# A grouped-query decode attention plus token mixer: ring of load buffers at multiples of 512 bytes, one output-weight load no longer split, values loaded right behind the next keys, the last two heads' output weights loaded last

## The chip, the cores and the metric

The kernel runs on one NeuronCore of a Trainium2 chip. The metric is the device time of one execution in microseconds (us). Several executions are timed; the median of three executions of the kernel before is 1326.07 us (1325.22 to 1327.07). One further execution is recorded by the hardware profiler. Engines are named as the profile names them: PE is the matrix engine (PEld its weight loads), DVE the vector engine, ACT the scalar engine, POOL the general engine, and SP the engine whose queue issues nearly all DMA transfers. All data is float32.

## The reference, cut to what matters

```python
B, Sq, D = 8, 1, 512
Hq, Hkv, Sk, Dh = 32, 8, 8192, 128          # k_cache, v_cache: (B, Hkv, Sk, Dh)
x = A_x
xn = _layernorm(x)
q = (xn @ wq).reshape(B, 1, 32, 128).transpose(0, 2, 1, 3)
k = jnp.repeat(k_cache, 4, axis=1)
v = jnp.repeat(v_cache, 4, axis=1)
p = softmax(einsum("bhqd,bhkd->bhqk", q, k) * 128 ** -0.5)
a = einsum("bhqk,bhkd->bhqd", p, v).transpose(0, 2, 1, 3).reshape(B, 1, 4096) @ wo
h = _layernorm(xn)                            # mixer: tokens axis has length 1
u = gelu(einsum("bsd,sf->bdf", h, w1) + b1)   # F = 1792
y = einsum("bdf,fs->bds", u, w2) + b2
return x + a + y.transpose(0, 2, 1)
```

Each of the 64 pairs of a key/value head h (8) and a batch b (8) has 4 MiB of keys and 4 MiB of values, and four query rows. The caches alone are 537 MB (512 MiB), wq and wo are 8 MiB each.

## The kernel before

The 64 pairs are numbered i = 8h + b, and one pass of `slot(i)` (line 361) works on one pair. A pair's keys, and likewise its values, are one tile `raw` of 128 partitions x 64 rows x 128 numbers (32 KiB in each partition, 4 MiB in all). These tiles live in the pool `ring`, which has five buffers that are used in turn: the sixth tile takes the first buffer, and its load can be issued only when the last reader of the old tile is done. In the text K62 means the keys of pair 62, V62 its values.

**What sets the order of the loads.** Lines 51 to 57 sort a list `order`: keys of pair i at 2i, values at 2i + 1, but for the last two pairs at 2i + 2.5. So the loads stand as K0, V0, K1, V1, ... V61, K62, K63, V62, V63. `load_next` (line 67) takes the next entry and issues it on SP's queue. It is called when a pair's keys have been used (end of `qk`, line 224) and when its values have been used (end of `pv`, line 271). SP works in order: an issue that waits for a buffer holds back those behind it. K0 and K63 are loaded in four pieces, V63 in four pieces of falling size, everything else in one.

**The output weights.** `wo` for head h (1 MiB, `load_wo`, line 83) is a tile of its own of 8 KiB per partition, loaded in the slot with b = 2 of head h. Head 6 is loaded in two transfers, partitions 0 to 7 and partitions 8 to 127 (line 87). Head 7 is loaded behind everything else, in four transfers (lines 79 and 91).

**A slot.** `qk(i)` is 16 matrix products (32 PE rows in the profile, since one float32 product runs as two) of the transposed keys with the placed queries W. DVE transposes the next pair's keys in four quarters, `turn(i + 1, ...)` (line 209), with the softmax of pair i between them: `sm_max` (DVE), `sm_bias` (PE and DVE), `sm_exp` (ACT), `sm_place` (PE, then DVE writes PT). PE does `pv(i - 1)` right behind `qk(i)`, then `o_pick` (three DVE operations that keep the right quarter and add it up) and `o_place` (PE, into the PSUM tile MH of the head). At b = 0 the previous head's result is scaled (`o_sums`, `o_scale`) and multiplied with wo (`o_project`, line 303). The mixer runs beside it on ACT and POOL (`mx_step`), and `mx_end` brings its sum in through PE.

**The end.** Slots 0 to 62 run in the loop; pair 63 is written out by hand from line 399: qk, softmax, pv(62), its pick and place, `o_sums`, pv(63), pick and place, scale, `o_project(7)`, and the store of `yacc`.

**Where the ring lies.** The pool `const` lies in front of the ring in each partition. In the built program the ring's first buffer begins at byte 36,736, which is 128 bytes past a multiple of 256 and 384 past a multiple of 512; the others follow at steps of 32,768.

## Time and profile before

| What | Before |
|---|---|
| Time, median of 3 | 1326.07 us |
| Time of the profiled execution | 1324.89 us |
| Its span (first to last instruction) | 1323.1 us |
| Busy: PE, DVE, ACT, POOL | 790.6, 806.1, 289.0, 230.9 us |
| Loaded by SP's queue (q1) | 553.67 MB in 24,331 packets |
| Mean granted clock of PE | 0.76 |

The span is 1.8 us shorter than the time of the same execution. Four views are used: the page with its 40 slices of 33.08 us each and its groups, the windows (busy time and DMA rate in chosen stretches), the chain of waits, and the timeline of the end. A row of the timeline gives start, duration, engine, source line, operation, output and inputs, how many instructions were merged, and in brackets the idle time in front and what ended it. In a row of the chain stand start, duration and what ran or was waited for. In the windows' rows stand the window, its length, the busy time and count of each engine, the granted clock, the mean busy share of the 16 DMA engines, and GB/s.

### The profile page before, as it was taken

Reading aid. Unit: us, or ns where it says so; the run is one execution under the profiler, and the core shown is the slowest. Engines: PE = TensorE matmul, PEld = TensorE weight load, DVE = VectorE, ACT = ScalarE, POOL = GpSimd, SP = SyncE. Lnnn points to the kernel's source line nnn. Section 1 sums busy time; section 2 is a strip of 40 time slices with the busy share of each in tenths; the row PEclk is TensorE's granted clock in tenths of the full one; section 3 lists DMA queues with packets and bytes.
Section 4 is the critical chain, followed back from the end, with each engine's and each line's share of the span. In section 5 each row is a group of like instructions: output and inputs, shape, how many; then the busy total and the mean of one; then the engine's idle time right before and its main releaser. Section 6 shows DMA issues by size and latency. Waiting matters only on the chain.

```text
span 1323.1 us, 12383 instructions
## 1 busy us (share of the span) xinstructions
PE 790.6 (60%) x5172; PEld 260.9 (20%) x5172; DVE 806.1 (61%) x835; ACT 289.0 (22%) x364; POOL 230.9 (17%) x244
## 2 busy tenths in 40 slices
PE   3366456655577466655467556576466663657566
PEld 2111112111121111211112111121112111122112
DVE  2655765746755666755755756655766736666563
ACT  0023212213212212213212213023221312213220
POOL 1022120212112121112112122022120221203310
PEclk9687786887777787787776776777776886767879
DMA  9999999999999999999999999999999999999993
GB/s 397 437 432 427 429 427 434 432 427 429 432 430 430 427 432 431 431 424 432 432 431 427 429 430 427 434 422 429 432 429 428 433 342 429 435 430 420 432 423 126
DMA packets 24530, 554.50 MB, mean 419 GB/s; under 512 B 2547, under 2 KB 2579, under 8 KB 6939
## 3 DMA queue, kind: packets, MB, share of 16 engines
q1 hardware_dynamic: 24331, 553.67, 98.2%
q8 instruction: 41, 0.67, 0.2%
q14 instruction: 14, 0.11, 0.0%
q0 software_dynamic: 128, 0.02, 0.0%
q10 hardware_dynamic: 16, 0.02, 0.0%
HBM read 553.69 MB, written 0.02 MB: 418 GB/s over the span
## 4 chain that ended last, share of the span: by engine, by line
DMA 53%; PE 22%; DVE 16%; issue 4%; ACT 4%; SPq 0%; ACTq 0%; DVEq 0%
DMA raw<-in_A_k_cache_dram 53%; DVE raw L212 13%; PE s L222 13%; PE misc L253 5%; ACT L246 2%; DVE mr L232 2%; ACT t2k L246 1%; PE misc L317 1%; PE misc L307 1%; PE misc L295 1%; PE o L266 1%; DVE t2k L277 1%; DVE sq L240 0%; PE mh L288 0%; DVE ob L280 0%
## 5 line engine op out<-in xcount | busy, mean ns | idle before, releaser
L212 DVE STREAM_TRANSPOSE raw<-raw 128x2048 f32<-128x2048 f32 x256 | 582.1, 2294 | 380.1 <-DMA raw<-in_A_k_cache_dram 380.1
L222 PE MATMUL s<-raw,w 128*32 128x512 f32 x2048 | 322.2, 785 | 17.0 <-issue 11.8
L328 POOL TENSOR_SCALAR g<-g,w2t 128x512 f32<-128x512 f32 x112 | 77.6, 693 | 921.8 <-ACT g L327 921.8
L266 PE MATMUL o<-raw,pt 128*32 128x512 f32 x2048 | 231.0, 592 | 0.0
L288 PE MATMUL mh<-sel,ob 128*128 128x4 f32 x128 | 35.6, 349 | 322.1 <-DVE ob L281 322.1
L246 ACT ACT_TABLE_LOAD x55 | 70.6, 1283 | 611.6 <-DVE nb L240 611.4
L329 POOL TENSOR_TENSOR macc<-macc,g 128x512 f32<-128x512 f32 x112 | 144.3, 1288 | 9.4
L253 PE MATMUL misc<-t2k,perm 128*128 128x512 f32 x128 | 125.4, 1080 | 15.6 <-ACT t2k L246 15.6
L222 PEld LDWEIGHTS s<-raw,w 128*32 128x32 f32 x2048 | 76.8, 143 | 275.5 <-issue 262.8
L237 PE MATMUL misc<-ident,mr 128*128 128x128 f32 x128 | 33.2, 343 | 146.1 <-DVE mr L232 146.1
L327 ACT ACTIVATE g<-hb,b1t,w1t 128x512 f32<-128x512 f32 x112 | 91.1, 813 | 128.7 <-POOL macc L329 128.0
L288 PEld LDWEIGHTS mh<-sel,ob 128*128 128x128 f32 x128 | 30.0, 291 | 336.6 <-DVE ob L281 336.6
L266 PEld LDWEIGHTS o<-raw,pt 128*32 128x32 f32 x2048 | 62.2, 110 | 157.8 <-issue 157.8
L246 ACT ACTIVATE t2k<-s,nb 128x512 f32<-128x512 f32 x64 | 44.0, 687 | 201.5 <-DVE nb L240 200.9
L255 DVE STREAM_TRANSPOSE pt<-misc 128x512 f32<-128x512 f32 x64 | 45.6, 712 | 39.7 <-PE misc L253 39.6
L327 ACT ACT_TABLE_LOAD x54 | 69.3, 1283 | 1.4
L237 PEld LDWEIGHTS misc<-ident,mr 128*128 128x128 f32 x128 | 20.2, 198 | 203.5 <-DVE mr L232 196.8
L232 DVE TENSOR_REDUCE mr<-s 128x1 f32<-128x512 f32 x64 | 42.0, 657 | 13.4 <-PE s L222 13.4
L277 DVE TENSOR_TENSOR t2k<-o,dm 128x512 f32<-128x512 f32 x64 | 43.9, 685 | 6.3 <-PE o L266 6.3
L205 DVE COPY w<-qt 32x128 f32<-32x128 f32 x64 | 37.1, 617 | 0.7
L253 PEld LDWEIGHTS misc<-t2k,perm 128*128 128x128 f32 x128 | 30.8, 299 | 20.0 <-ACT t2k L246 20.0
L280 DVE TENSOR_TENSOR ob<-t2k 128x256 f32<-128x256 f32 x64 | 27.2, 425 | 2.2
(67 smaller groups left out, 197.5 us busy)
## 6 DMA issues: line engine op xcount, KB each, us to landing
raw<-in_A_v_cache_dram SPq DMA_DIRECT2D x63, 4096.0 KB, 28.9
raw<-in_A_k_cache_dram SPq DMA_DIRECT2D x62, 4096.0 KB, 22.6
raw<-in_A_wq_dram SPq DMA_DIRECT2D x2, 4096.0 KB, 17.1
raw<-in_A_k_cache_dram SPq DMA_DIRECT2D x8, 1024.0 KB, 24.3
wo<-in_A_wo_dram SPq DMA_DIRECT2D x6, 1024.0 KB, 29.9
raw<-in_A_v_cache_dram SPq DMA_DIRECT2D x1, 2048.0 KB
raw<-in_A_v_cache_dram SPq DMA_DIRECT2D x1, 1024.0 KB, 25.8
raw<-in_A_v_cache_dram SPq DMA_DIRECT2D x2, 512.0 KB, 26.8
```

Source lines behind the costliest of these rows:

```text
L212: nc.vector.transpose(t, t)
L222: nc.tensor.matmul(S[i][g * Q:(g + 1) * Q, :], W[h % 2][:, b, j, :], kt[:, g, :, j * Q:(j + 1) * Q], start=(j == 0), stop=(j == NB - 1))
L232: nc.vector.tensor_reduce(mr, S[i], AX.X, ALU.max)
L237: nc.tensor.matmul(m[:, :P], st[i].to_broadcast([P, P]), ident, start=True, stop=True)
L246: nc.scalar.activation(p, S.pop(i), AF.Exp, bias=st[i], scale=SCALE, accum_out=LR[h % 2][:, b:b + 1])
L253: nc.tensor.matmul(m, perm, st.pop(i), start=True, stop=True)
L266: nc.tensor.matmul(O[i][c * Q:(c + 1) * Q, :], PT[i][:, u * Q:(u + 1) * Q], VR[i][:, u * NG:(u + 1) * NG, :].rearrange("p t d -> p (t d)") ...
L277: nc.vector.tensor_tensor(om.rearrange("p (g d) -> p g d", g=NG), O.pop(i).rearrange("p (g d) -> p g d", g=NG), dm.unsqueeze(2).to_broadca ...
L288: nc.tensor.matmul(MH[h][:, b * REP:(b + 1) * REP], OB.pop(i)[:, :DH], sel, start=True, stop=True)
L327: nc.scalar.activation(g, hb, AF.Gelu_apprx_tanh, bias=b1t[:, j:j + 1], scale=w1t[:, j:j + 1])
L328: nc.gpsimd.tensor_scalar(g, g, w2t[:, j:j + 1], 1.0, op0=ALU.mult, op1=ALU.mult)
L329: nc.gpsimd.tensor_add(acc, acc, g)
```

## The change

The load order becomes K0, K1, V0, K2, V1, ... with every pair's values behind the next pair's keys; near the end it is V60, K62, K63, V61, V62, V63. K63 is no longer cut in four. The output weights of heads 6 and 7 are no longer loaded into the `wo` tile: behind V63 they go into one ring buffer, in eight transfers of 256 KiB, and `o_project(6)` leaves slot 56 and is joined to `o_project(7)` at the end. The split load of head 6 goes with that. Pair 62 leaves the loop: the end is written out by hand for pairs 62 and 63, with pv(61), pv(62) and pv(63) behind qk(63). The last pair's pick and place become `o_last`: half of O copied by DVE and half by ACT, then four products with `selg`, a new constant that holds the pick and the place together. `mx_end` of the last head moves from slot 62 to slot 61. Two constants come in front of the ring, `selg` (64 bytes per partition) and `pad` (64 bytes, set to zero and read by nothing), so that the ring begins at byte 36,864 = 72 x 512.

```diff
--- before.py
+++ after.py
@@ -27,6 +27,7 @@
 SCALE = DH ** -0.5
 N_IT = B * HKV
 RING = 5
+PAD = 16
 
 
 @with_exitstack
@@ -51,8 +52,8 @@
     KR, VR = {}, {}
     order = []
     for i in range(N_IT):
-        order.append((2 * i, kc, KR, i))
-        order.append((2 * i + (1 if i < N_IT - 2 else 2.5), vc, VR, i))
+        order.append((2 * min(i, N_IT - 1.9), kc, KR, i))
+        order.append((2 * i + 2.5, vc, VR, i))
     order.sort(key=lambda o: o[0])
     order.reverse()
     WQ = []
@@ -71,24 +72,24 @@
             t = ring.tile([P, NT, DH], F32, name="raw")
             rows = src[b, h].rearrange("(p t) d -> p t d", p=P)
             at = 0
-            for n in (NT // 4,) * 4 if to is KR and i in (0, N_IT - 1) else (NT // 2, NT // 4, NT // 8, NT // 8) if not order else (NT,):
+            for n in (NT // 4,) * 4 if to is KR and i == 0 else (NT // 2, NT // 4, NT // 8, NT // 8) if not order else (NT,):
                 nc.sync.dma_start(t[:, at:at + n, :], rows[:, at:at + n, :])
                 at += n
             to[i] = t
-            if not order:
-                load_wo(HKV - 1)
+        elif HKV - 1 not in wos:
+            t = ring.tile([P, NT, DH], F32, name="raw")
+            t = t.rearrange("p (h r c) d -> p h r (c d)", h=4, r=REP)
+            for h in (HKV - 2, HKV - 1):
+                rows = wo[h * REP * DH:(h + 1) * REP * DH, :].rearrange("(r p) n -> p r n", p=P)
+                wos[h] = t[:, h % 2]
+                for r in range(REP):
+                    nc.sync.dma_start(wos[h][:, r, :], rows[:, r, :])
 
     wos = {}
 
     def load_wo(h):
         t = one.tile([P, REP, D], F32, name="wo")
-        rows = wo[h * REP * DH:(h + 1) * REP * DH, :].rearrange("(r p) n -> p r n", p=P)
-        if h < HKV - 1:
-            for p in (slice(0, 8), slice(8, P)) if h == HKV - 2 else (slice(0, P),):
-                nc.sync.dma_start(t[p], rows[p])
-        else:
-            for r in range(REP):
-                nc.sync.dma_start(t[:, r, :], rows[:, r, :])
+        nc.sync.dma_start(t, wo[h * REP * DH:(h + 1) * REP * DH, :].rearrange("(r p) n -> p r n", p=P))
         wos[h] = t
 
     load_wq()
@@ -126,6 +127,8 @@
                           ident.rearrange("p (g i x) -> p i g x", i=NB, g=NG))
     dm = const.tile([P, NG], F32, name="dm")
     nc.vector.tensor_reduce(dm, ident.rearrange("p (c g x) -> p g c x", c=NB, g=NG), AX.XY, ALU.add)
+    selg = const.tile([P, NG, REP], F32, name="selg")
+    nc.vector.tensor_tensor(selg, sel.unsqueeze(1).to_broadcast([P, NG, REP]), dm.unsqueeze(2).to_broadcast([P, NG, REP]), ALU.mult)
     rj = const.tile([P, NB, NB, Q], F32, name="rj")
     nc.vector.tensor_copy(rj, ident.rearrange("p (j d) -> p j d", j=NB).unsqueeze(2).to_broadcast([P, NB, NB, Q]))
     epst = const.tile([B, 1], F32, name="epst")
@@ -146,6 +149,9 @@
         nc.vector.memset(t, 0.0)
         OTS.append(t)
         LR.append(const.tile([P, B], F32, name=f"lr{k}"))
+
+    pad = const.tile([P, PAD], F32, name="pad")
+    nc.vector.memset(pad, 0.0)
 
 
 
@@ -287,6 +293,16 @@
             MH[h] = ps_h.tile([P, 512], F32, name="mh")
         nc.tensor.matmul(MH[h][:, b * REP:(b + 1) * REP], OB.pop(i)[:, :DH], sel, start=True, stop=True)
 
+    def o_last(i):
+        om = t2k.tile([P, 512], F32, name="t2k")
+        o = O.pop(i)
+        nc.vector.tensor_copy(om[:, :256], o[:, :256])
+        nc.scalar.copy(om[:, 256:], o[:, 256:])
+        b = i % B
+        for g in range(NG):
+            nc.tensor.matmul(MH[i // B][:, b * REP:(b + 1) * REP], om[:, g * DH:(g + 1) * DH], selg[:, g, :],
+                             start=(g == 0), stop=(g == NG - 1))
+
     RD = {}
 
     def o_sums(h):
@@ -300,12 +316,15 @@
         nc.vector.tensor_tensor(OTS[h % 2].rearrange("p r (b s) -> p r b s", s=BS)[:, :, :, 0],
                                 MH.pop(h)[:, :REP * B].rearrange("p (b r) -> p r b", r=REP), RD.pop(h), ALU.mult)
 
-    def o_project(h):
-        m = misc()
-        for r in range(REP):
-            for j in range(NB):
-                nc.tensor.matmul(m[j * Q:(j + 1) * Q, :D // NB], OTS[h % 2][:, r, :], wos[h][:, r, quarter[j]],
-                                 start=(r == 0), stop=(r == REP - 1))
+    def o_project(*hs):
+        m = misc()
+        n = 0
+        for h in hs:
+            for r in range(REP):
+                n += 1
+                for j in range(NB):
+                    nc.tensor.matmul(m[j * Q:(j + 1) * Q, :D // NB], OTS[h % 2][:, r, :], wos[h][:, r, quarter[j]],
+                                     start=(n == 1), stop=(n == REP * len(hs)))
         nc.vector.tensor_add(yacc, m[:, :D // NB], yacc)
 
 
@@ -380,26 +399,39 @@
             if h:
                 o_sums(h - 1)
                 o_scale(h - 1)
-                o_project(h - 1)
+                if h + 1 < HKV:
+                    o_project(h - 1)
         k = 2 if h + 1 < HKV else 3
         for j in range(k * b, min(k * b + k, NF)):
             mx_step(h, j)
-        if b == 2 and h + 1 < HKV:
+        if b == 2 and h + 2 < HKV:
             load_wo(h)
         if 3 <= b < 3 + NB and h + 1 < HKV:
             q_place(h + 1, b - 3)
-        if b == (B - 1 if h + 1 < HKV else B - 2):
+        if b == (B - 1 if h + 1 < HKV else B - 3):
             mx_end(h)
 
     for a in range(4):
         turn(0, a * quart)
-    for i in range(LAST):
+    for i in range(LAST - 1):
         slot(i)
     h = HKV - 1
+    qk(LAST - 1)
+    turn(LAST, 0)
+    sm_max(LAST - 1)
+    turn(LAST, quart)
+    sm_bias(LAST - 1)
+    sm_exp(LAST - 1)
+    turn(LAST, 2 * quart)
+    sm_place(LAST - 1)
+    turn(LAST, 3 * quart)
     qk(LAST)
     sm_max(LAST)
     sm_bias(LAST)
     sm_exp(LAST)
+    pv(LAST - 2)
+    o_pick(LAST - 2)
+    o_place(LAST - 2)
     sm_place(LAST)
     pv(LAST - 1)
     o_pick(LAST - 1)
@@ -407,10 +439,9 @@
     o_sums(h)
     for u0, u1 in ((0, 8), (8, 12), (12, 14), (14, 16)):
         pv(LAST, u0, u1)
-    o_pick(LAST)
-    o_place(LAST)
+    o_last(LAST)
     o_scale(h)
-    o_project(h)
+    o_project(h - 1, h)
     nc.sync.dma_start(out.rearrange("b s (j n) -> j (b s) n", j=NB), yacc[::BS, :])
 
 
```

The first place is SP's queue at the start of the program; `raw` is a buffer of the ring, with the tile's number. Before:

```order
L64 DMA raw_86<-in_A_wq_dram 128x8192
L75 DMA raw_96<-in_A_k_cache_dram 128x2048 x4
L75 DMA raw_101<-in_A_v_cache_dram 128x8192
L75 DMA raw_103<-in_A_k_cache_dram 128x8192
L75 DMA raw_349<-in_A_v_cache_dram 128x8192
L75 DMA raw_351<-in_A_k_cache_dram 128x8192
```

And of the change:

```order
L65 DMA raw_86<-in_A_wq_dram 128x8192
L76 DMA raw_96<-in_A_k_cache_dram 128x2048 x4
L76 DMA raw_101<-in_A_k_cache_dram 128x8192
L76 DMA raw_103<-in_A_v_cache_dram 128x8192
L76 DMA raw_353<-in_A_k_cache_dram 128x8192
L76 DMA raw_355<-in_A_v_cache_dram 128x8192
```

K1 now stands ahead of V0, and so on to the end of the list. With five buffers, K of pair i + 2 used to take the buffer of V of pair i - 1, and now V of pair i + 1 takes that of K of pair i.

The second place is the end of SP's queue, from the keys of pair 61 on. Before:

```order
L75 DMA raw_4735<-in_A_k_cache_dram 128x8192
L75 DMA raw_4758<-in_A_v_cache_dram 128x8192
L75 DMA raw_4808<-in_A_k_cache_dram 128x8192
L75 DMA raw_4831<-in_A_k_cache_dram 128x2048 x4
L75 DMA raw_4880<-in_A_v_cache_dram 128x8192
L75 DMA raw_4903<-in_A_v_cache_dram 128x4096
L75 DMA raw_4903<-in_A_v_cache_dram 128x2048
L75 DMA raw_4903<-in_A_v_cache_dram 128x1024 x2
L91 DMA wo_4908<-in_A_wo_dram 128x512 x4
L414 DMA out_0_dram<-yacc_94 4x8x128
```

Of the change, from the same keys on:

```order
L76 DMA raw_4668<-in_A_k_cache_dram 128x8192
L76 DMA raw_4718<-in_A_v_cache_dram 128x8192
L76 DMA raw_4741<-in_A_k_cache_dram 128x8192
L76 DMA raw_4791<-in_A_k_cache_dram 128x8192
L76 DMA raw_4814<-in_A_v_cache_dram 128x8192
L76 DMA raw_4860<-in_A_v_cache_dram 128x8192
L76 DMA raw_4883<-in_A_v_cache_dram 128x4096
L76 DMA raw_4883<-in_A_v_cache_dram 128x2048
L76 DMA raw_4883<-in_A_v_cache_dram 128x1024 x2
L86 DMA raw_4930<-in_A_wo_dram 128x512 x8
L445 DMA out_0_dram<-yacc_94 4x8x128
```

Between K61 and K62 stands V60 instead of V61, V61 stands behind K63, and eight weight transfers close the queue where four did.

The third place is PE's end, from the qk of pair 62 on (s is the score tile, o the output of pv, mh the head's collected outputs). Before:

```order
L222 MATMUL s_4932<-raw_4808,w1_141 32x512 x16
L266 MATMUL o_4953<-raw_4758,pt_4930 32x512 x16
L237 MATMUL misc_4971<-ident_109,mr_4950 128x128
L288 MATMUL mh_4624<-sel_120,ob_4978 128x4
L253 MATMUL misc_4985<-t2k_4982,perm_122 128x512
L334 MATMUL misc_4989<-macc_4531,bsel_130 32x128 x4
L222 MATMUL s_4995<-raw_4831,w1_141 32x512 x16
L237 MATMUL misc_5014<-ident_109,mr_5012 128x128
L253 MATMUL misc_5021<-t2k_5019,perm_122 128x512
L266 MATMUL o_5025<-raw_4880,pt_4987 32x512 x16
L288 MATMUL mh_4624<-sel_120,ob_5044 128x4
L295 MATMUL misc_5048<-lr1_145,sel_120 128x8 x4
```

Of the change, from the mixer's sum on, which now stands ahead of qk(62):

```order
L353 MATMUL misc_4907<-macc_4532,bsel_132 32x128 x4
L228 MATMUL s_4913<-raw_4741,w1_143 32x512 x16
L243 MATMUL misc_4943<-ident_109,mr_4940 128x128
L259 MATMUL misc_4951<-t2k_4948,perm_122 128x512
L228 MATMUL s_4956<-raw_4791,w1_143 32x512 x16
L243 MATMUL misc_4975<-ident_109,mr_4973 128x128
L272 MATMUL o_4982<-raw_4814,pt_4905 32x512 x16
L294 MATMUL mh_4607<-sel_120,ob_5001 128x4
L259 MATMUL misc_5005<-t2k_4980,perm_122 128x512
L272 MATMUL o_5009<-raw_4860,pt_4953 32x512 x16
L294 MATMUL mh_4607<-sel_120,ob_5028 128x4
L311 MATMUL misc_5032<-lr1_147,sel_120 128x8 x4
```

pv(61) moved from between qk(62) and its softmax to behind qk(63), and the placing of pair 63's probabilities (L259) moved behind it. Behind these rows stand pv(63), four products of `o_last` in place of one, and 32 products with wo in place of 16.

## The prediction

> **What bounds the kernel now.** The page's slices come first: loading runs at some 430 GB/s in nearly all of them. Then the page's chain by line, and the costliest group.
>
> ```profile
> GB/s 397 437 432 427 429 427 434 432 427 429 432 430 430 427 432 431 431 424 432 432 431 427 429 430 427 434 422 429 432 429 428 433 342 429 435 430 420 432 423 126
> DMA raw<-in_A_k_cache_dram 53%; DVE raw L212 13%; PE s L222 13%; PE misc L253 5%; ACT L246 2%; DVE mr L232 2%; ACT t2k L246 1%; PE misc L317 1%; PE misc L307 1%; PE misc L295 1%; PE o L266 1%; DVE t2k L277 1%; DVE sq L240 0%; PE mh L288 0%; DVE ob L280 0%
> L212 DVE STREAM_TRANSPOSE raw<-raw 128x2048 f32<-128x2048 f32 x256 | 582.1, 2294 | 380.1 <-DMA raw<-in_A_k_cache_dram 380.1
> ```
>
> DVE waits 380.1 us for keys, so no engine sets the pace; the transfers do. Two places stand out: slice 33 with 342 GB/s, and the last slice, where loading is over while the program still runs. The windows show the first place against the long stretches on both sides, and then the last stretch of loading.
>
> ```profile
> 60.00:1060.00 1000.00, 612.20 (x3816) 196.65 (x3820) 627.19 (x627) 231.64 (x288) 179.57 (x184) 0.75 1.00 430
> ...
> 1068.00:1088.00 20.00, 11.90 (x70) 3.47 (x70) 10.57 (x13) 4.97 (x6) 4.03 (x4) 0.74 1.02 286
> ...
> 1100.00:1290.00 190.00, 117.41 (x736) 37.35 (x740) 123.03 (x121) 46.45 (x58) 39.99 (x41) 0.74 1.00 428
> ...
> 1296.00:1300.00 4.00, 3.44 (x25) 1.06 (x28) 1.86 (x3) 0.00 (x0) 0.00 (x0) 0.60 0.84 330
> 1300.00:1304.00 4.00, 2.79 (x22) 0.70 (x14) 0.94 (x3) 0.00 (x0) 0.00 (x0) 0.97 0.29 109
> ```
>
> At 1068 to 1088 us the DMA engines are as busy as elsewhere (1.02) but move a third less: (430 - 286) / 430 x 20 = 6.7 us lost. At the end loading stops near 1303 us, 20 us ahead of the span's end. The rows of the DMA issues (size, time from issue to landing) and of the weights' issues say what lies at both places.
>
> ```profile
> raw<-in_A_v_cache_dram SPq DMA_DIRECT2D x63, 4096.0 KB, 28.9
> raw<-in_A_k_cache_dram SPq DMA_DIRECT2D x62, 4096.0 KB, 22.6
> ...
> wo<-in_A_wo_dram SPq DMA_DIRECT2D x6, 1024.0 KB, 29.9
> ...
> wo<-in_A_wo_dram SPq DMA_DIRECT2D x1, 960.0 KB, 38.8
> ...
> L88 SPq DMA_DIRECT2D wo<-in_A_wo_dram x8: 330/428/616, 94.0 to 1047.6; - x8
> L91 SPq DMA_DIRECT2D wo<-in_A_wo_dram x4: 328/328/328, 1275.7 to 1290.4; - x4
> ...
> DMA to landing us min/median/max: 12.5/28.7/38.8
> ```
>
> The 960 KB piece is the larger half of head 6's split load. It was issued at 1047.6 and took 38.8 us, up to 1086, so it lay in the slow stretch; the six whole loads, 29.9 us each, show no such stretch. The last quarter of head 7 landed at 1290.4 + 12.5 = 1302.9.
>
> **The change: up to the keys of pair 62.** I follow the moment at which K62 has landed, since everything behind it is one chain. The chain of waits gives the cadence; each row is the first transposition of a pair's keys, which starts when these have landed.
>
> ```profile
> 887.95 2.31 DVE raw L212
> ...
> 929.53 2.31 DVE raw L212
> ...
> 1007.22 2.31 DVE raw L212
> ...
> 1046.07 2.31 DVE raw L212
> ...
> 1095.91 2.31 DVE raw L212
> ...
> 1134.78 2.31 DVE raw L212
> ```
>
> These are two pairs apart. Plain: 1046.07 - 1007.22 = 38.85 us for four tiles, 9.71 us a tile. With a whole wo load among them: 41.58, so such a load costs 2.73. With the split one: 49.84, so 10.99, of which 8.26 is the split. Behind it the cadence is 38.87 again: nothing is caught up. I take 8.26, as the landing of the slowest part counts; 6.7 (the windows) is the other end.
>
> In the new order K62 has one tile less ahead of it (V61 moves behind it) and no weights of head 6: 9.71 + 10.99 = 20.70 us earlier. K62 landed at 1270.76 (first row below), and so at **1250.06**.
>
> The reordering itself I cost at nothing, because the order of equal transfers doesn't change their sum as long as the queue never runs dry. In the new order each issue waits for a buffer that the operation just ended sets free. K of pair i + 3 is issued behind pv(i - 1), with three tiles (29 us) still to come ahead of it; V of pair i + 1 is issued behind qk(i), with some 22 us ahead. Before, the keys had only one tile ahead. Nothing but loads stands behind a waiting issue on SP. V of pair i lands 9.7 us after K of pair i + 1, and pv(i) starts some 16 us after it (rows below: 1270.76 to 1287.93 for pair 61), so values come in time, also behind a wo load (2.73).
>
> The ring at multiples of 512 bytes I cost at nothing as well. No row shows a load into an aligned ring; the nearest rows are slices at 420 and 437 GB/s, which as a rate for the whole way to K62 (1250 us at 430) would be +29 and -20 us; two long windows, 430 and 428, differ by 6 us on that way. I take 0, nearest to the long windows, and keep 6 us each way. The set-up of `selg` and `pad` is two small DVE operations ahead of the first keys.
>
> ```profile
> 31.07 0.88 DVE L197 COPY qt<-misc 128x128 f32<-128x128 f32 x4 [15.08 <-PE misc L194]
> ```
>
> DVE then stands idle for 15 us until PE has the queries, which hides them; uncovered they would cost about as much as one such copy, 0.2 us each.
>
> **The change: behind K62.** The timeline of the end, in its present order, and one row of the groups (busy us, mean ns):
>
> ```profile
> 1270.76 2.31 DVE L212 STREAM_TRANSPOSE raw<-raw 128x2048 f32<-128x2048 f32 x1 [6.93 <-DMA raw<-in_A_k_cache_dram]
> 1282.45 5.66 PE L222 MATMUL s<-raw,w 128*32 128x512 f32 x32
> 1287.93 3.61 PE L266 MATMUL o<-raw,pt 128*32 128x512 f32 x32
> 1296.20 0.43 PE L334 MATMUL misc<-macc,bsel 128*32 128x128 f32 x8
> 1297.19 5.12 PE L222 MATMUL s<-raw,w 128*32 128x512 f32 x32 [0.56 <-PE misc L334]
> 1303.12 0.49 PE L237 MATMUL misc<-ident,mr 128*128 128x128 f32 x2 [0.81 <-DVE mr L232]
> 1304.91 1.12 PE L253 MATMUL misc<-t2k,perm 128*128 128x512 f32 x2 [1.31 <-ACT t2k L246]
> 1305.97 3.64 PE L266 MATMUL o<-raw,pt 128*32 128x512 f32 x32
> ...
> 1306.08 0.72 DVE L255 STREAM_TRANSPOSE pt<-misc 128x512 f32<-128x512 f32 x1 [2.03 <-PE misc L253]
> 1311.28 0.39 PE L288 MATMUL mh<-sel,ob 128*128 128x4 f32 x2 [1.67 <-DVE ob L281]
> 1311.52 1.04 PE L295 MATMUL misc<-lr,sel 128*128 128x8 f32 x8
> 1312.49 3.64 PE L266 MATMUL o<-raw,pt 128*32 128x512 f32 x32
> ...
> 1316.99 0.42 DVE L280 TENSOR_TENSOR ob<-t2k 128x256 f32<-128x256 f32 x1
> 1317.80 0.39 PE L288 MATMUL mh<-sel,ob 128*128 128x4 f32 x2 [1.67 <-DVE ob L281]
> 1318.49 1.08 PE L307 MATMUL misc<-wo,ot 128*32 128x128 f32 x32 [0.30 <-DVE ot L300]
> 1319.96 0.67 SPq L414 DMA_DIRECT2D out_dram<-yacc  x1
> ...
> L185 ACT COPY t2k<-s 128x512 f32<-128x512 f32 x2 | 1.2, 586 | 22.1 <-PE s L182 22.1
> ```
>
> Before, from K62 on: qk(62) at +11.69, qk(63) at +26.43, pv(62) at +35.21, pv(63) at +41.73, the end at +52.34. After the change:
>
> - `mx_end` stands ahead of qk(62): it took 0.99 from its start to the next qk (1296.20 to 1297.19), so qk(62) starts at +12.7 and ends at +18.3.
> - From the end of qk(62) to the start of qk(63) it was 1288.11 to 1297.19, 9.1: DVE's max, three quarters of K63, the bias, and the pick of pair 61. The pick goes (1.67 with its gaps: pv's end 1309.61 to the place at 1311.28), and the transposition to PT comes in (0.72), with gaps 8.6. qk(63) starts at +26.9 and ends, 5.12 later, at +32.1. K63 unsplit costs nothing: it lands at +9.7, DVE comes to it at +12.4; without that cover it would be three quarters of a tile, 7.3 us.
> - Max and bias of pair 63: 1297.19 + 5.12 = 1302.31 to 1303.61, 1.3: PE is free at +33.4.
> - pv(61) with its pick and place, now here: 1305.97 to 1311.49, 5.52; then L259 1.1: +40.0.
> - pv(62), pick, place 5.5 and the sums 1.0: pv(63) starts at **+46.5** instead of +41.73, ends at +50.1. Its values have landed: K63, V61, V62, V63 are four tiles behind K62, +38.9.
> - `o_last`: before, pv's end 1316.13 to the end of the place 1318.19, 2.06. The copy of half of O is bounded by DVE's add of the same shape (0.42) and half of ACT's copy of a whole tile (0.3); eight products are priced as the eight of the sums (1.04). With the gaps 1.7: 0.4 saved.
> - Scale as before, 0.3. `o_project` twice as long: 64 rows for 32, 1.08 more. The rest as before: 1319.57 to 1323.1, 3.5.
>
> The sum behind K62: 50.1 + 1.7 + 0.3 + 2.16 + 3.5 = 57.8 instead of 52.34, **5.5 us longer**. The weights land two wo loads (5.5) behind V63, at +44.4, and are needed at +52.1: 7.7 us to spare.
>
> Span: 1250.06 + 57.8 = 1307.9. The profiled execution took 1324.89 for a span of 1323.1, so 1.8 lie outside: 1309.7. The median of the runs shown is 1.2 above the profiled one, so up to 1310.9. I predict **1310**.
>
> **The rivals.** *The aligned ring is loaded faster.* Each 32 KiB row begins 128 bytes off, so it may touch one more block of memory than it must. For it: the long windows (430) stay under the best slice (437). Against it: a slice holds whole rows only by chance, and other slices lie as far below. Half of that gap is 0.8%, 10 us: 1300.
> The Trainium skill (“DMA: Bandwidth & Descriptors”, “How a descriptor splits into AXI transactions”) says that transfers are cut at 256-byte boundaries and that a start off a boundary costs beats for bytes not used, which it tells of reads. By that rule 128 bytes are 4 beats on 1,024, as an estimate 0.4% or 5 us, which would make it 1305; no run here shows it for a write.
>
> *The split was not the cause.* Something else slowed the transfers at 1068 us and will do so again: then 8.3 us come back, 1318. For it: only one split load exists, so one coincidence would do. Against it: the place fits to a few us.
>
> *The weights become the bound.* Eight pieces of 256 KiB may not run at full rate: in the last window before, with four such pieces, it was 109 GB/s. At that rate 2 MiB take 19 us from +38.9, to +58, 6 us past the need: 1316. Against it: most of that window is idle time at the end of unequal engines, and only the last pieces suffer.
>
> *Slower: the ring at 512 is loaded worse.* All five buffers and every row then begin at the same place modulo 512 with the engines' own reads. At 420 GB/s, as in the slowest undisturbed slice, it is +29 us, 1339; below 424 GB/s, 16 us, the whole gain is gone. Against it: nothing in the trace ties a slow slice to a place.
>
> **How the numbers follow.** Forecast 0.66 (1304 to 1316, from the 6 us of the rate); faster ring 0.10; split not the cause 0.12; weights 0.05; slower ring 0.04; no difference for a reason that I don't see 0.03. The range 1302 to 1319 leaves out the slower ring, no difference, and half of the faster ring, about 0.12, and a little at the edges. Faster by over 0.2% (what a measurement of this kernel can tell from no change) is 0.66 + 0.10 + 0.12 + 0.05 = 0.93, slower 0.04, the same 0.03.
>
> **What would show it.** No slice between the first and the last two below 415 GB/s, else the split wasn't the cause. Median time to landing near 38 us for keys and 32 for values (four or three tiles queued), instead of 22.6 and 28.9. K62's first transposition near 1250, qk(63) 27 us behind it, pv(63) near 1296.5 with no idle PE ahead of it that a transfer ends; 64 products with wo in about 2.2 us, started by DVE's scale and not by a DMA. Wrong I would be if long windows show another rate than 428 to 430, or if PE waits for values.

## The result, and the profile after

The changed kernel takes 1304.41 us (median of 4 runs, 1303.8 to 1304.5). The kernel before, timed on the same chip, takes 1326.57 us (median of 4 runs, 1325.22 to 1327.11). The ratio is 0.9833 with an interval of 0.9816 to 0.9851: 1.7% faster, 5.6 us below the forecast of 1310 and inside its range. The profiled execution took 1303.8 us for a span of 1301.9 us.

The page of the kernel after: slices of loading, the chain by line, the costliest group, and the DMA issues (KB of one, median us from issue to landing).

```profile
GB/s 403 434 434 428 429 434 431 434 432 431 431 432 435 430 434 433 431 430 430 434 431 433 433 432 428 434 433 431 430 432 433 432 435 432 435 432 430 429 432 216
DMA raw<-in_A_k_cache_dram 56%; DVE raw L218 10%; PE s L228 10%; PE o L272 6%; PE misc L259 3%; ACT L252 2%; DMA raw<-in_A_wq_dram 2%; DVE mr L238 1%; ACT t2k L252 1%; PE s L188 1%; PE misc L336 1%; PE misc L326 1%; PE misc L311 0%; DVE t2k L283 0%; DVE sq L246 0%
...
L218 DVE STREAM_TRANSPOSE raw<-raw 128x2048 f32<-128x2048 f32 x256 | 582.1, 2294 | 347.8 <-DMA raw<-in_A_k_cache_dram 347.8
raw<-in_A_k_cache_dram SPq DMA_DIRECT2D x63, 4096.0 KB, 38.2
raw<-in_A_v_cache_dram SPq DMA_DIRECT2D x63, 4096.0 KB, 32.0
...
raw<-in_A_wo_dram SPq DMA_DIRECT2D x8, 256.0 KB, 7.3
```

Slice 33 with its 342 GB/s is gone: between the first and the last slice nothing lies below 428. The slices scatter less, too (428 to 435, where those before, slice 33 and the last apart, went from 420 to 437). DVE still waits for keys and for nothing else that counts, 347.8 us instead of 380.1: the transfers are the bound as before. The windows say how fast they are now (the last columns are the granted clock, the DMA share and GB/s).

```profile
60.00:1060.00 1000.00, 617.66 (x3870) 198.19 (x3870) 634.46 (x634) 232.61 (x290) 181.65 (x186) 0.76 1.00 432
1068.00:1088.00 20.00, 12.66 (x93) 3.75 (x88) 13.28 (x13) 4.97 (x6) 4.63 (x5) 0.83 1.00 430
1100.00:1240.00 140.00, 89.25 (x520) 27.73 (x524) 88.96 (x86) 37.15 (x47) 33.52 (x35) 0.74 1.00 433
1280.00:1284.00 4.00, 2.33 (x24) 0.57 (x14) 1.41 (x3) 0.00 (x0) 0.00 (x0) 1.00 0.77 286
1284.00:1288.00 4.00, 4.00 (x32) 1.28 (x36) 0.72 (x1) 0.00 (x0) 0.00 (x0) 1.00 0.80 301
1288.00:1292.00 4.00, 2.40 (x22) 1.35 (x18) 1.75 (x4) 0.00 (x0) 0.00 (x0) 1.00 0.19 71
```

Two things were not in the forecast. The long stretches run at 432 and 433 GB/s; before, the first of them ran at 430 and the stretch from 1100 to 1240 us at 429. Another rate than 428 to 430 was a sign that the prediction had named for being wrong. And in the windows from 1280 to 1288 us, close to the end of loading, the rate is 286 and 301 GB/s, with the DMA engines busy to 0.77 and 0.80. The rows of the weights' issues tell more about this (the first gives the times of the first and the last issue):

```profile
L86 SPq DMA_DIRECT2D raw<-in_A_wo_dram x8: 327/328/431, 1262.3 to 1284.8; - x8
...
DMA to landing us min/median/max: 5.1/7.3/21.4
```

The last of the eight pieces was issued at 1284.8 us, and the quickest landed 5.1 us after its issue, where a whole tile in the full queue took 32 to 38 us. SP had waited for values to land ahead of most of these issues (six waits, 20.0 us in all). This fits engines that have little issued work left in these windows; whether they also finish at different times is not shown. The timeline of the end (start, duration, engine, line, operation, and in brackets the idle time in front with what ended it) begins at K62's first transposition.

```profile
1246.04 2.31 DVE L218 STREAM_TRANSPOSE raw<-raw 128x2048 f32<-128x2048 f32 x1 [6.88 <-DMA raw<-in_A_k_cache_dram]
...
1258.16 4.02 PE L228 MATMUL s<-raw,w 128*32 128x512 f32 x32
...
1271.30 5.97 PE L228 MATMUL s<-raw,w 128*32 128x512 f32 x32 [3.00 <-DVE raw L218]
...
1278.51 3.64 PE L272 MATMUL o<-raw,pt 128*32 128x512 f32 x32
...
1285.10 3.64 PE L272 MATMUL o<-raw,pt 128*32 128x512 f32 x32
...
1291.56 3.64 PE L272 MATMUL o<-raw,pt 128*32 128x512 f32 x32
...
1295.81 1.05 PE L303 MATMUL mh<-selg,t2k 128*128 128x4 f32 x8 [0.62 <-DVE t2k L299]
...
1296.80 1.95 PE L326 MATMUL misc<-raw,ot 128*32 128x128 f32 x64
1296.90 0.22 DVE L316 TENSOR_TENSOR ot<-mh,rd 128x32 f32<-128x32 f32 x1 [1.15 <-PE mh L303]
...
1299.14 0.69 SPq L445 DMA_DIRECT2D out_dram<-yacc  x1
```

K62 lands 24.72 us earlier than before (1270.76 to 1246.04), and what follows takes 55.86 us (1301.9 - 1246.04) instead of 52.34. None of the engines' waits behind K62 ends with a transfer: the last DMA wait of the chain is the 6.88 us in its first row.

### The profile page after: what moved, and what is told of

Its sections match the earlier page's. It is cut to its first block, busy times and chain, and to the rows that moved or that the text cites. A ratio compares the mean times of both kernels' runs of the same rounds, so it can differ in the third digit from the quotient of the medians.

```text
span 1301.9 us, 12448 instructions
## 1 busy us (share of the span) xinstructions
PE 791.1 (61%) x5178; PEld 260.6 (20%) x5178; DVE 805.8 (62%) x834; ACT 289.4 (22%) x365; POOL 231.0 (18%) x244
## 4 chain that ended last, share of the span: by engine, by line
DMA 58%; PE 22%; DVE 13%; issue 4%; ACT 3%; SPq 0%; ACTq 0%; DVEq 0%
DMA raw<-in_A_k_cache_dram 56%; DVE raw L218 10%; PE s L228 10%; PE o L272 6%; PE misc L259 3%; ACT L252 2%; DMA raw<-in_A_wq_dram 2%; DVE mr L238 1%; ACT t2k L252 1%; PE s L188 1%; PE misc L336 1%; PE misc L326 1%; PE misc L311 0%; DVE t2k L283 0%; DVE sq L246 0%
## 5 line engine op out<-in xcount | busy, mean ns | idle before, releaser
L218 DVE STREAM_TRANSPOSE raw<-raw 128x2048 f32<-128x2048 f32 x256 | 582.1, 2294 | 347.8 <-DMA raw<-in_A_k_cache_dram 347.8
L259 PE MATMUL misc<-t2k,perm 128*128 128x512 f32 x128 | 125.0, 1077 | 17.2 <-ACT t2k L252 17.2
L259 PEld LDWEIGHTS misc<-t2k,perm 128*128 128x128 f32 x128 | 30.7, 297 | 21.6 <-ACT t2k L252 21.6
## 6 DMA issues: line engine op xcount, KB each, us to landing
raw<-in_A_k_cache_dram SPq DMA_DIRECT2D x63, 4096.0 KB, 38.2
raw<-in_A_k_cache_dram SPq DMA_DIRECT2D x4, 1024.0 KB, 26.9
```

Source lines behind the costliest of these rows:

```text
L218: nc.vector.transpose(t, t)
L259: nc.tensor.matmul(m, perm, st.pop(i), start=True, stop=True)
```

## The experiments

The 22.2 us can come from three places: where the ring lies, the split load, and the order of the last loads with the rewritten end. My theory after the result was that the ring's address, priced at nothing, is worth the 4 to 6 us that the forecast lacks. The rival was that the new load order feeds the queue better all the way. "Before" stands for runs of the kernel before on the same chip; its medians were 1326.07, 1326.15, 1325.98 and 1326.89 us in the four groups of runs.

**The ring's address alone, in the kernel before (b_align).** 128 bytes more in the pool in front move the ring from byte 36,736 to 36,864, and the pools behind it too.

```diff
@@ kernel before, behind the constants
+    pad = const.tile([P, 32], F32, name="pad")
+    nc.vector.memset(pad, 0.0)
```

> The kernel before with one edit: 128 bytes of padding per partition in front of the ring, so that its buffers begin at multiples of 512. Nothing else is moved. If the address sets the rate of the loads: four tiles take 38.73 us as after the change, instead of 38.85, K62 lands some 4 us earlier and the time is 1322.5; the slow stretch at 1068 us stays. If the changed order (a deeper queue) gave the rate: no change, 1326.5, cadence 38.85.

Median 1319.55 us (1318.87 to 1321.28), ratio 0.9952 (0.9939 to 0.9966). The long stretch in the windows, in the kernel before and then in b_align, and K62's row in b_align's chain of waits:

```profile
60.00:1040.00 980.00, 600.11 (x3742) 193.12 (x3746) 615.45 (x616) 226.67 (x282) 175.57 (x180) 0.75 1.00 430
```

```profile
60.00:1040.00 980.00, 599.30 (x3766) 193.31 (x3770) 615.79 (x616) 227.45 (x283) 177.46 (x182) 0.76 1.00 432
```

```profile
1265.47 2.31 DVE raw L215
```

With the order, the split and the end of before, K62 lands 5.29 us earlier (from 1270.76), and the long stretch runs at 432. The address is a cause by itself, and it is worth 0.5%, more than the 4 us expected. The slow stretch at 1068 us stays (304 GB/s), so the two causes are separate.

**The address taken back, in the kernel after (a_mis128), and a multiple of 256 that is none of 512 (a_256).** PAD counts 4-byte words; 48 puts the ring at 36,992 (128 past a multiple of 512), 80 at 37,120 (256 past).

```diff
@@ kernel after, a_mis128
-PAD = 16
+PAD = 48
@@ kernel after, a_256
-PAD = 16
+PAD = 80
```

> The changed kernel with 128 bytes more of padding: the ring begins at byte 36,992, 128 past a multiple of 512. If the address sets the rate: cadence 38.85 for four tiles, K62 lands 4 us later, 1308.4. If the order did it: 1304.4, cadence 38.73.

> The changed kernel with 256 bytes more of padding: the ring begins at byte 37,120, a multiple of 256 but not of 512. If blocks of 256 bytes matter, this is as good as the change: 1304.4, cadence 38.73. If blocks of 512 matter, it is as slow as 128 bytes off: 1308.4, cadence 38.85. If the address doesn't matter: 1304.4.

a_mis128: 1309.91 us (1309.22 to 1310.26), ratio to before 0.9879 (0.9866 to 0.9893). a_256: 1304.5 us (1303.99 to 1304.88), ratio 0.9839 (0.9825 to 0.9852). Their long stretches in the windows, a_mis128 first:

```profile
60.00:1040.00 980.00, 599.46 (x3800) 193.76 (x3800) 618.17 (x616) 227.42 (x283) 177.55 (x182) 0.76 1.00 430
```

```profile
60.00:1040.00 980.00, 605.21 (x3800) 195.41 (x3800) 624.22 (x624) 228.38 (x284) 177.45 (x182) 0.76 1.00 432
```

Moved by 128 bytes, the changed kernel loses 5.5 us and falls back to 430 GB/s with its own order of loads, so the order is not what gives the rate. At 256 past a multiple of 512 nothing is lost: a multiple of 256 is enough.

**Does the price grow with the distance from the boundary? (a_off192)** PAD = 64 puts the ring 192 bytes past a multiple of 256.

```diff
@@ kernel after
-PAD = 16
+PAD = 64
```

> The changed kernel with the ring 192 bytes past a multiple of 256 instead of 0 (128 past it cost 5.5 us). If a row that starts off the boundary pays for the bytes between the boundary and its start (4 beats at 128 bytes, 6 at 192): 1.5 times as much, 8.2 us, 1312.6, and a cadence of 38.92 for four tiles. If it pays once for one piece more, however far off it starts: 1309.9 as at 128, cadence 38.86.

1310.45 us (1310.13 to 1310.78), ratio 0.9883 (0.987 to 0.9897). The chain's rows for K62 in a_off192 and then in a_mis128:

```profile
1251.53 2.31 DVE raw L218
```

```profile
1251.63 2.31 DVE raw L218
```

The same landing at 192 as at 128, 5.5 us behind 1246.04. So the price does not grow with the distance, between these two at least. With 130 loads of 4 MiB (64 of keys, 64 of values, 2 of wq), 128 rows each and 16 DMA engines, an engine moves 1,040 rows, and 5.5 us on them are an estimated 5.3 ns a row. The traces also keep the time of every single row's transfer. From 60 to 1040 us, 99% of the 32 KiB rows took 1213 ns in the kernel after and in a_256; in a_mis128 only 21% did and in a_off192 only 6%, with nearly all others up to 1227. The means are 1214.5, 1214.5, 1218.7 and 1218.6 ns. These 4 ns a row are most of the loss, so it lies in the transfers themselves and not in gaps between them. It is a mean: the rows do not all pay the same, and why they pay is not shown.

The Trainium skill (“DMA: Bandwidth & Descriptors”, “How a descriptor splits into AXI transactions”) counts a price by the bytes between the 256-byte boundary below and the start, for reads. The estimate worked out from it for 128 bytes (5 us) has the measured size, and its boundary of 256 is the one seen here. But by that rule 192 bytes would cost half as much again, which the trace does not show, and the address that moved here is the one written.

**The split alone (b_nosplit).** The kernel before with head 6's weights in one transfer.

```diff
@@ kernel before, load_wo
-            for p in (slice(0, 8), slice(8, P)) if h == HKV - 2 else (slice(0, P),):
+            for p in (slice(0, P),):
```

> The kernel before with one edit: head 6's output weights are loaded in one transfer. If the split costs what the chain of waits showed: 8.3 us less, 1318.3, and the two pairs around the load take 41.6 us instead of 49.8. By the bytes lost in the window it would be 6.7 us less, 1319.8. If the slow stretch at 1068 us had another cause it comes back: 1326.5.

1318.88 us (1317.24 to 1320.34), ratio 0.9948 (0.9935 to 0.996). The two keys' rows of the chain around that load, and the window of the slow stretch:

```profile
1045.73 2.31 DVE raw L212
...
1088.57 2.31 DVE raw L212
```

```profile
1068.00:1088.00 20.00, 12.11 (x70) 3.50 (x70) 10.51 (x13) 4.97 (x6) 4.02 (x4) 0.74 1.03 435
```

42.84 us for the two pairs instead of 49.84, and 435 GB/s instead of 286. The split was the cause of the slow stretch, and it cost 7.0 us there. The rival "the split was not the cause" is out.

**What about the split is slow: uneven shares (b_split16), or two transfers (b_splitr)?** The one cuts at partition 16 instead of 8, so that both pieces (16 and 112 partitions) divide by 16; the other makes two transfers of all 128 partitions with half of each row.

```diff
@@ kernel before, load_wo, b_split16
-            for p in (slice(0, 8), slice(8, P)) if h == HKV - 2 else (slice(0, P),):
+            for p in (slice(0, 16), slice(16, P)) if h == HKV - 2 else (slice(0, P),):
@@ kernel before, load_wo, b_splitr
-            for p in (slice(0, 8), slice(8, P)) if h == HKV - 2 else (slice(0, P),):
-                nc.sync.dma_start(t[p], rows[p])
+            for r in (slice(0, 2), slice(2, 4)) if h == HKV - 2 else (slice(0, REP),):
+                nc.sync.dma_start(t[:, r, :], rows[:, r, :])
```

> The kernel before, with head 6's weights split at partition 16 instead of 8, so that both transfers (16 and 112 partitions) can be shared evenly among 16 DMA engines. If the split was slow because 8 and 120 partitions leave engines out: as good as one transfer, 1318.9, the two pairs around the load take 42.8 us. If it was slow because a transfer that doesn't cover all 128 partitions has its engines write to other partitions than they do otherwise, and so get in each other's way: slow as before, 1326, 49 to 50 us.

> The kernel before, with head 6's weights in two transfers that both cover all 128 partitions (the first two and the last two of the four rows of each). If two transfers instead of one were the cost: 1326. If only transfers over part of the partitions are slow: as with one transfer, 1318.9, and 42.8 us for the two pairs around the load.

b_split16: 1326.38 us (11 runs, 1323.64 to 1327.43), ratio 0.9999 (0.999 to 1.0008). b_splitr: 1319.47 us (1318.74 to 1320.66), ratio 0.9953 (0.9941 to 0.9966). The windows, b_split16 first:

```profile
1068.00:1088.00 20.00, 11.08 (x70) 3.29 (x70) 10.84 (x13) 4.97 (x6) 4.03 (x4) 0.74 1.03 307
```

```profile
1068.00:1088.00 20.00, 11.27 (x70) 3.33 (x70) 10.49 (x13) 4.98 (x6) 4.03 (x4) 0.74 1.03 432
```

Two transfers cost nothing as long as each covers all partitions. A cut across the partitions stays slow at 16 as at 8. Within these four kernels the partial cover is what decides, not the number of transfers.

In the slow stretch the engines' busy share is 1.03 as in the fast one, so they are not idle. The times of the single rows show what happens. In the kernel before, the weights of head 6 move from 1070.5 to 1085.4 us, in 14.9 us; in b_nosplit they take 7.9. Meanwhile a 32 KiB row of the caches takes 2.21 us (median) in before and 1.92 in b_split16, but 1.22 in b_nosplit and in b_splitr; a 2 KiB row of the weights takes 0.17 and 0.16 us, but 0.09 in the other two. The partial transfers are slow themselves and slow the rows that move beside them. This fits the second guess, that the engines get in each other's way; what they compete for was not settled.

The Trainium skill (“DMA: Bandwidth & Descriptors”, “Why a DMA increments its semaphore by 16 and not by 1”) has a transfer spread over as many engines, up to 16, as divide the slowest dimension of both its sides. By that rule the cut at 16 uses all 16 engines for both pieces; the 307 GB/s say that the count of engines is not the whole matter.

**Both edits in the kernel before (b_both).** The edits of b_align and b_nosplit together.

```diff
@@ kernel before
-            for p in (slice(0, 8), slice(8, P)) if h == HKV - 2 else (slice(0, P),):
+            for p in (slice(0, P),):
...
+    pad = const.tile([P, 32], F32, name="pad")
+    nc.vector.memset(pad, 0.0)
```

> The kernel before with both single edits: the padding that puts the ring at multiples of 512, and head 6's weights in one transfer; order and end as before. Alone they gave -6.5 and -7.2 us. If they act on different stretches and add up: 1312.4, and the remaining 8 us to the changed kernel belong to the order of the last loads and the rewritten end. If they overlap: above 1313.5.

1313.4 us (1312.38 to 1314.24), ratio 0.9903 (0.9889 to 0.9917): 1.0% below before, and the two single gains add up to 1.0% (0.48 and 0.52). What is left to the changed kernel, 1313.4 - 1304.41 = 9.0 us, belongs to the order of the last loads, the place of head 6's weights and the new end.

**Values ahead of the next keys again, but for the last three pairs (a_oldorder).**

```diff
@@ kernel after, the load order
-        order.append((2 * i + 2.5, vc, VR, i))
+        order.append((2 * i + (1 if i < N_IT - 3 else 2.5), vc, VR, i))
```

> The changed kernel with the old order of loads for pairs 0 to 60 (values of pair i right behind its own keys) and the new order only at the end. If the reordering is worth nothing while the queue never runs dry: 1304.4, cadence 38.73 for four tiles, and the times to landing go back to some 23 us (keys) and 29 us (values). If the deeper queue gave part of the gain: slower, by up to 2 us for the part of the gain that the address and the split leave open.

1309.3 us (1308.37 to 1309.83), ratio 0.9874 (0.9861 to 0.9888): 4.9 us slower than the changed kernel, which I had not expected. Its long stretch in the windows, then its timeline at K61, K62 and qk(62), and then K61's row in the timeline of the kernel after:

```profile
60.00:1040.00 980.00, 600.34 (x3782) 193.39 (x3786) 615.13 (x616) 227.50 (x283) 177.79 (x182) 0.75 1.00 432
```

```profile
1236.51 2.31 DVE L218 STREAM_TRANSPOSE raw<-raw 128x2048 f32<-128x2048 f32 x1 [6.81 <-DMA raw<-in_A_k_cache_dram]
...
1248.95 2.27 DVE L218 STREAM_TRANSPOSE raw<-raw 128x2048 f32<-128x2048 f32 x1
...
1262.80 4.67 PE L228 MATMUL s<-raw,w 128*32 128x512 f32 x32
```

```profile
1226.65 2.31 DVE L218 STREAM_TRANSPOSE raw<-raw 128x2048 f32<-128x2048 f32 x1 [6.87 <-DMA raw<-in_A_k_cache_dram]
```

K61 lands one tile later (9.86 us), since V60 now stands ahead of it, and DVE comes to K62 at 1248.95 without waiting for a transfer: the chain no longer starts at K62's landing, but at K61's, with DVE's work on it in between. qk(62) starts 4.64 us later and takes 0.65 longer, and the span ends 5.6 us later (1307.5 and 1301.9). Over the long way the old order costs nothing, at the same 432 GB/s: K61 lands 9.86 us later, of which one tile is 9.7. The times to landing go back to 22.2 us for keys and 28.3 for values without a price. The last pairs make the difference, and the rival that the new order feeds the queue better all the way is out.

**V61 ahead of K62 again (a_v61).**

```diff
@@ kernel after, the load order
-        order.append((2 * i + 2.5, vc, VR, i))
+        order.append((2 * i + (1.5 if i == N_IT - 3 else 2.5), vc, VR, i))
```

> The changed kernel with V61 loaded ahead of K62 again, as before the change; K62, K63, V62, V63 and the weights follow. If the end hangs on the landing of K62: K62 lands one tile, 9.7 us, later, and the time is 1314.1. If the end hangs on the last loads (which end as before): 1304.4.

1314.2 us (1313.57 to 1314.83), ratio 0.9912 (0.9898 to 0.9925). K62's row in its timeline:

```profile
1255.59 2.31 DVE L218 STREAM_TRANSPOSE raw<-raw 128x2048 f32<-128x2048 f32 x1 [16.48 <-DMA raw<-in_A_k_cache_dram]
```

K62 lands 9.55 us later and the end comes 9.8 us later: one tile ahead of K62 is one tile of time. a_v61 has the rewritten end and both heads' weights at the end, and yet stands where b_both stands (1314.2 and 1313.4): without V61's new place these two bring nothing. K62 lands 3.2 us earlier in a_v61 than in b_both (1255.59 and 1258.79), and what follows it takes 3.0 us longer (56.7 and 53.7). In this program they are worth having because V61 can only go behind the last keys if pv(61) goes behind qk(63).

**One tile more behind the last keys (a_keys2, a_keys3).** V60 goes behind K63 too, so that K61, K62 and K63 follow each other. a_keys2 takes pair 61 out of the loop, with pv(60) and its pick behind qk(62).

```diff
@@ kernel after, a_keys2
-        order.append((2 * min(i, N_IT - 1.9), kc, KR, i))
+        order.append((2 * min(i, N_IT - 3 + 0.1 * (i - N_IT + 3)), kc, KR, i))
...
-    for i in range(LAST - 1):
+    for i in range(LAST - 2):
...
+    i = LAST - 2
+    qk(i)
...
     qk(LAST - 1)
+    pv(i - 1)
+    o_pick(i - 1)
+    o_place(i - 1)
     turn(LAST, 0)
     sm_max(LAST - 1)
```

> The changed kernel taken one step further: V60 as well is loaded behind K62 and K63, pair 61 is written out by hand too, and pv(60) stands behind qk(62). If the end hangs on the landing of K62: it lands at 1236.3, 9.7 us earlier; pv(60) with its pick and place adds 3.6 to 5.5 us to the chain, so the time is 1299 to 1301. The last weights land at some 1289.5, and 2 us of products, the add and the store (3.4) behind them make a floor of 1295 for the span. If the end hangs on the last loads already: 1304.4.

1304.86 us (1304.77 to 1305.59), ratio 0.9843 (0.9829 to 0.9856): no gain on the changed kernel, against the 1299 to 1301 expected. The timeline of a_keys2 says where it went.

```profile
1256.40 3.61 PE L272 MATMUL o<-raw,pt 128*32 128x512 f32 x32
...
1260.15 0.69 DVE L283 TENSOR_TENSOR t2k<-o,dm 128x512 f32<-128x512 f32 x1 [7.83 <-PE o L272]
...
1261.55 2.30 DVE L218 STREAM_TRANSPOSE raw<-raw 128x2048 f32<-128x2048 f32 x1
...
1272.84 6.22 PE L228 MATMUL s<-raw,w 128*32 128x512 f32 x32 [3.00 <-DVE raw L218]
```

DVE stands for 7.83 us at the pick of pair 60, with K63's transpositions and the softmax of pair 62 queued behind it, so qk(63) starts at 1272.84, no earlier than the 1271.30 of the changed kernel. The wait for keys had become a wait for pv(60). a_keys3 changes only the order on PE and DVE: the pick goes behind the softmax's max and bias of pair 62. In pair 61, the third quarter of K62 also goes behind the softmax's bias and exp; qk(62) starts no earlier for that (1252.03 us, and 1251.73 in a_keys2).

```diff
@@ a_keys2 to a_keys3
...
     qk(LAST - 1)
-    pv(i - 1)
-    o_pick(i - 1)
-    o_place(i - 1)
     turn(LAST, 0)
...
     sm_exp(LAST - 1)
+    pv(i - 1)
     turn(LAST, 2 * quart)
+    o_pick(i - 1)
     sm_place(LAST - 1)
     turn(LAST, 3 * quart)
+    o_place(i - 1)
```

> V60 behind K62 and K63 once more, but with the work of the end in another order on DVE: K63's first two quarters and the max and bias of pair 62 stand ahead of the pick of pair 60, and pv(60) behind the bias of pair 62. If the step before gained nothing because DVE stood in the pick's wait and the softmax behind transpositions: qk(63) starts some 5 us earlier than after the change, at 1266 instead of 1271, and the time is 1299 to 1300. If the last loads hold the end: 1304, with PE waiting for a transfer ahead of the last pv or of the products with wo.

1300.54 us (1299.63 to 1301.59), ratio to before 0.981 (0.9796 to 0.9823): below both kernels. Its timeline, at the same places:

```profile
1257.22 0.69 DVE L238 TENSOR_REDUCE mr<-s 128x1 f32<-128x512 f32 x1 [2.90 <-PE s L228]
...
1262.46 0.65 DVE L283 TENSOR_TENSOR t2k<-o,dm 128x512 f32<-128x512 f32 x1
...
1266.77 6.28 PE L228 MATMUL s<-raw,w 128*32 128x512 f32 x32 [2.43 <-DVE raw L218]
```

The pick no longer waits, qk(63) starts 4.53 us ahead of the changed kernel's, and the span ends 4.3 us earlier (1297.6 and 1301.9).

## Why the prediction was right in kind and 5.6 us too high

**The address of the ring: the term that was mis-sized.** The step "The ring at multiples of 512 bytes I cost at nothing" took 0 of a range of 6 us each way. Measured, it is 5.5 us (a_mis128) to 6.5 (b_align): the edge of the range, and half of the price of the rival "the aligned ring is loaded faster". I weighed 430 against 437 GB/s in single slices, where a slice holds whole rows only by chance; long windows of one kernel cannot show the price of an address that never changes in it. It is as large as the miss, and that the miss is no larger or smaller is luck: the other errors, 1.4 us too much gain for head 6's weights (by difference) and 1.9 too much time for the end, nearly cancel.

**The split: right, and a little too large.** 8.26 us were predicted, 7.0 (cadence in b_nosplit) to 7.2 (its time) measured. The 2.73 us of a whole load came from places with other neighbours; at this place it takes 42.84 - 38.85 = 4.0. The 6.7 us of the windows, the other end that I kept, were as near.

**V61 behind K62: right.** 9.71 predicted, 9.55 measured (a_v61). Together: K62 was to land 20.70 us earlier and landed 24.72 earlier. With 5.6 us for the address (K62 in a_mis128 against after) and 9.55 for V61, some 9.6 are left for head 6's weights, where the sum had 10.99. This 9.6 is only what is left over: the rows at that place give 7.0 + 4.0 = 11.0, so it is open whether this term was too large.

**The reordering at nothing: right for the long way, incomplete at the end.** The times to landing are 38.2 and 32.0 us where I had named 38 and 32, and with the old order over the first 61 pairs the transfers are no slower. But the sum let the chain start at K62's landing, and this holds only because K61 no longer waits for V60; a_oldorder shows what that cover is worth, 4.9 us. It was inside the sum, without being named.

**The end: 57.8 us predicted, 55.86 measured.** By its steps, counted from K62's first transposition:

| Step | Predicted | Measured |
|---|---|---|
| qk(62) starts | +12.7 | +12.12 |
| qk(62) ends | +18.3 | +16.14 |
| qk(63) starts | +26.9 | +25.26 |
| pv(61) starts | +33.4 | +32.47 |
| pv(63) starts | +46.5 | +45.52 |
| products with wo start | +52.1 | +50.76 |
| end of the span | +57.8 | +55.86 |

At the end of qk(62) 2.2 us have been gained: it started 0.6 earlier and took 4.02 us instead of 5.66. The windows of just these stretches, before and after, show the same work at another granted clock, 0.64 and 0.90, which the forecast could not know:

```profile
1282.45:1288.11 5.66, 5.66 (x37) 1.45 (x40) 2.91 (x2) 0.00 (x0) 0.00 (x0) 0.64 0.95 408
```

```profile
1258.16:1262.18 4.02, 4.02 (x39) 0.92 (x28) 2.81 (x3) 0.00 (x0) 0.00 (x0) 0.90 0.98 424
```

qk(63) took 5.97 instead of the 5.12 taken for it and gave 0.85 of that back. From the end of qk(62) to the start of qk(63) it is 9.1 us where I had 8.6. By pv(63) 1.0 us is left. `o_last`, from the end of pv(63) at 1295.20 to that of its products at 1296.86, took the 1.7 it was given. The last 1.0 comes behind it: the 64 products with wo took 1.95 us and not 2.16, and began at 1296.80, right behind the products of `o_last` and ahead of the scale at 1296.90. Head 6's half does not wait for that scale, so the 0.3 us that I had counted for it lie beside the products; the prediction had the scale start them. From the end of the products to the end of the span it is 3.15 us (1298.75 to 1301.9) instead of 3.5.

**The rivals.** Weights as the bound: out. The rate did fall at the end (286, 301, then 71 GB/s; the late issues of the pieces are one reason, where the prediction spoke of unequal engines), but loading stops in the window that ends at 1292, at least 4.8 us ahead of the products with wo at 1296.80. Worse loading at 512: out, with the opposite sign.

## What to carry to other kernels

Where a kernel is bound by its loads, place the destination buffers at multiples of 256 bytes in the partition, and let every transfer in a full queue cover all partitions: here each is worth 0.5% and costs a line or two. Put in front of the last loads only what the longest chain of work needs, and then check the order on the engines for a wait that takes the place of the transfer's, as a_keys2 had one and a_keys3 did not. A term that no row of the trace can show because it is the same all over the kernel is not a term of zero; its bounds belong in the range.

## What the runs showed of the hardware that I had not expected

- The address to which rows of 32 KiB are written counts: 128 and 192 bytes past a multiple of 256 cost the same 5.5 to 6 us in 1304, and 256 past a multiple of 512 costs nothing. Single rows took 1213 ns in 99% of cases at a multiple of 256, and from 1213 to some 1225 off it.
- A load of 1 MiB cut across the partitions (8 and 120, or 16 and 112) brought a stretch of 20 us down to 286 and 307 GB/s and cost 7 us, 0.7 of the time of a whole 4 MiB tile (9.71); cut along the rows it cost nothing. The rows of other transfers beside it took 1.92 to 2.21 us instead of 1.22.
- From 1280 to 1288 us, close to the end of loading, the DMA engines are busy to 0.77 and 0.80, at 286 and 301 GB/s, while the last small transfers are still being issued (until 1284.8).
- The same 32 products of qk took 4.02 us at a granted clock of 0.90 and 5.66 at 0.64, in stretches where the other engines did much the same: time times clock is 3.62 us in both.
